# An FFT filter with a top-128 feed-forward: x kept by halves of the channels, VectorE without folds and weight splits, a new order

## The chip, the cores and the metric

The kernel runs on one core of a Trainium2 chip. The metric is the device time in microseconds (us) of one execution.

## The reference

`x` is [8, 3136, 256] in f32: 8 batches, 3136 tokens, 256 channels. All in f32:

```
X = rfft(x, axis=1);  Y = X * (filt_r + 1j*filt_i);  y = irfft(Y)
scores = y @ w_gate                             # one per token
for each batch: idx = the 128 tokens of the highest score
  xe = y[idx]; ye = relu(xe @ w1) @ w2          # 256 -> 1024 -> 256
  y[idx] = xe + sigmoid(scores[idx]) * ye
```

## The kernel before, in words

**The transform.** 3136 = 98 * 32, and the FFT is done as two small DFTs by matmul. The tile `X` holds one batch, 98 rows (on 113 partitions: two groups of 49, at partitions 0 and 64) by 32 by 256 channels. It is the only such tile: it takes the loaded `x`, and later the result `y` of the batch before, in halves of 128 channels. The work is staged thus, with the names of the code:

- `load` (SP, lines 591 to 598): one half of `x` from DRAM, in two DMAs, of 112 partitions (L595) and of the one that is left (L596).
- the fold (L435): the symmetry of the DFT is used by forming sum and difference of two halves of a row, for one chunk of 32 channels at a time, 8 chunks a batch. The string `FOLD` has for each batch and chunk two letters, for the sum and for the difference: `p` on GpSimd (POOL), `d` on VectorE (DVE), `x` no fold: TensorE (PE) adds both operands in PSUM, with two more matmuls.
- `amm` (PE, L461): DFT over the 98. `tout` (DVE, L465): a 32x32 transpose out of PSUM into the tile `UU`.
- `inner`, for 13 pairs of rows: `zmm` (PE, L364) DFT over the 32; `zout` (ScalarE, ACT, L382) and `pmul` (DVE, L386), `qmul` (POOL, L389): product with the filter tables `fa_sb` and `fb_sb`; `vmm` (PE, L373): the inverse with `ti_sb`; `vout` (ACT, L398) back into `UU`; `gate` (DVE, L404): the scores.
- `tin` (DVE, L426) transposes back, `ymm` (PE, L567) is the last inverse DFT, `yout` (ACT, L570) writes into `X`, `store` (SP, L584, L587, L589) writes a half to DRAM.

`inner` of batch t runs beside the way out of batch t-1 and the way in of batch t+1. So a half of `X` is written by `yout`, stored, loaded anew and folded, in a ring.

**The selection** (`select`) finds the 128 tokens of a batch by 8 rounds of counting: ACT counts (L675), PE adds up (L684), and `over` works out the next bound, on ACT (L698, L699) or, where `SELM` of the batch is 1, on DVE (L692, L694).

**The feed-forward** (`ffn`) gathers the tokens, in four groups of batches; three of the groups multiply with weights in two f32r parts. The parts are made in 8 pieces, the upper by ACT (L872), the lower by a subtraction (L875) on POOL for the pieces in `WPOOL`, else on DVE. At the end indirect DMAs on POOL write the rows back (L987).

**Start.** The filter tables arrive in four parts (`PARTS`, L1040) and are copied to a second set of partitions by `spread` (L1047) on the engines in `SPR`; `turn_ti` (L1074, L1076) makes the second half of `ti_sb`. `warmup` (L1068) issues 2 * 34 matmuls on zeros (`WARM=34`).

**What sets the order.** Every step is appended to `prog` by `op(when, engine, cost, fn, reads, writes)`, but only the list `ORDER` counts: the steps are issued in its order (L1147), and each engine and SP's queue run theirs in that order, waiting on semaphores where a step needs data. `when`, `cost` and `lat` are a planner's figures (us); the kernel itself doesn't use them.

Of the kernel before, what the change touches and what calls it, by code (L numbers as in the profile page):

```python
# [9 lines left out]
F32 = mybir.dt.float32  # L10
# [7 lines left out]
B, S, D, FF = 8, 3136, 256, 1024  # L18
# [26 lines left out]
def _tables(C):  # L45
# [45 lines left out]
    for r in range(8):  # L91
# [10 lines left out]
    ti = ti.transpose(4, 1, 2, 3, 0, 5).reshape(128, NPR * 128)  # L102
# [20 lines left out]
    ],  # L123
    BACK=["ffffffff", "ffffffff", "ffffffff", "ffffffff", "ffffffff", "ffffffff", "peqeqqhq", "ppppffff"],
    BRING=["yyzzzzza", "yyzyzyza", "yyzzzzya", "aazzavza", "yyzzyvza", "aazzyyzy", "aaaaaaaa", "azvazava"],
    YRING=[
        "yymyyymyyyyyyyyy",
        "yyyyyyyyyyyyyyyy",
        "yyyyyyyyyyyyyyyy",
        "yyyyyyyyyyyyyyyy",  # L130
        "yyyyyyyyyyyyyyyy",
        "yyyyymyyyyyyyymy",
        "myymyymyyymymmym",
        "mmmymymyyyyyyymy",
# [3 lines left out]
        ["act", "pool", "act", "dve"],  # L138
        ["pool", "pool", "dve", "dve"],
        ["pool", "act", "dve", "dve"],  # L140
    ],
    SELM=[0, 0, 0, 0, 0, 1, 1, 1],
    WPOOL=[3, 6, 1, 4, 2],
# [105 lines left out]
]  # L249


# [928 lines left out]
```

## Time and profile before

| | us |
|---|---|
| median of 3 runs | 499.3 (492.7 to 499.85) |
| the profiled execution | 495.63 |
| its span, first to last instruction | 493.8 |

The rows below come from the profiled execution. Busy time is what the profiler records for each engine; matmul ends are modelled. A line number is that of the kernel before. In the span's first 60 us the first batches and the tables come in, to about 372 us the batches follow each other in a period of about 45 us, and the rest is the last way out, the last selections and the feed-forward.

### The profile page before, as it was taken

To read this page: it belongs to the slowest core of one execution; us is meant where nothing else is said; L and a number is where in the kernel's file an instruction comes from. 1 tells how busy PE (TensorE), PEld (TensorE's weight loads), DVE (VectorE), ACT (ScalarE), POOL (GpSimd) and SP (SyncE) were. 2 spreads that over 40 slices of the span, in tenths; PEclk is the share of its full clock that TensorE was granted. 3 is DMA by queue.
4 is the path that set the end of the run, shared out by engine and by line. 5 is a ranking of instruction groups with operands and counts; after the bars stand their busy time and mean duration, and the time that the engine had idled before them with its cause. 6 is when DMAs were issued, how large, how long until landed. Compare 5 with 4: busy or idle time off the path is not lost.

```text
span 493.8 us, 10471 instructions
## 1 busy us (share of the span) xinstructions
PE 439.3 (89%) x3876; PEld 223.3 (45%) x3876; DVE 404.7 (82%) x1062; ACT 276.9 (56%) x665; POOL 303.0 (61%) x257
## 2 busy tenths in 40 slices
PE   4847788999799999999999899989997979699996
PEld 4214342543244434343443244424433545368995
DVE  0699987999598989898999888989998997857642
ACT  1243423678356677457766675757666558466320
POOL 0678888663667459656966677657864654652023
PEclk9698998999899999999999999999999999899999
DMA  9999386117682828474758384758222465416411
GB/s 193 255 294 218 75 177 145 42 49 192 173 182 78 201 70 203 98 204 102 180 138 205 91 195 105 195 141 210 75 72 69 128 152 170 127 34 143 140 44 44
DMA packets 116856, 69.22 MB, mean 140 GB/s; under 512 B 3782, under 2 KB 115142, under 8 KB 116550
## 3 DMA queue, kind: packets, MB, share of 16 engines
q1 hardware_dynamic: 116038, 66.46, 55.9%
q0 software_dynamic: 768, 2.10, 1.3%
q8 instruction: 31, 0.51, 0.4%
q14 instruction: 19, 0.16, 0.1%
HBM read 41.61 MB, written 26.94 MB: 139 GB/s over the span
## 4 chain that ended last, share of the span: by engine, by line
PE 44%; DVE 18%; DMA 13%; issue 7%; POOL 7%; ACT 3%; SPq 0%; POOLq 0%; DVEq 0%; ACTq 0%
PE pv L373 12%; PE py L567 11%; DMA X<-in_x_dram 11%; PE pa L461 6%; PE pz L364 6%; DVE rj L404 5%; DVE y L386 3%; DVE t L426 2%; POOL q L389 2%; DMA out_dram<-X 2%; DVE UU L465 2%; POOL s L435 2%; POOL X L435 2%; ACT UU L398 1%; POOL out_dram L987 1%
## 5 line engine op out<-in xcount | busy, mean ns | idle before, releaser
L389 POOL TENSOR_TENSOR q<-q,fb_sb 128x512 f32<-128x512 f32 (+1 forms) x104 | 135.2, 1317 | 54.5 <-ACT q L382 51.2
L567 PE MATMUL py<-t,c_sb 128*98 128x512 f32 x198 | 109.0, 633 | 3.2 <-ACT X L570 2.9
L435 POOL TENSOR_TENSOR s<-X 113x512 f32<-113x512 f32 x48 | 63.2, 1325 | 70.3 <-DMA X<-in_x_dram 60.6
L404 DVE SCALAR_TENSOR_TENSOR rj<-pv,wg_sb 128x256 bf16<-128x256 f32 x200 | 83.8, 419 | 12.4 <-ACT UU L398 4.4
L461 PE MATMUL pa<-X,c_sb 49*64 49x512 f32 x320 | 77.6, 647 | 10.9 <-DMA c_sb<-in_cst_dram 5.6
L398 ACT COPY UU<-pv 128x512 f32<-128x512 f32 x96 | 51.7, 589 | 57.9 <-PE pv L373 57.4
L426 DVE STREAM_TRANSPOSE t<-UU 128x1024 f32<-128x1024 f32 x64 | 78.7, 1231 | 4.0 <-PE pm L684 3.4
L465 DVE STREAM_TRANSPOSE UU<-pa 128x1024 f32<-128x1024 f32 x59 | 73.2, 1240 | 6.9 <-PE pa L461 6.7
L570 ACT COPY X<-py 98x512 f32<-98x512 f32 x99 | 57.6, 582 | 36.7 <-PE py L567 15.8
L373 PE MATMUL pv<-y,ti_sb 64*64 64x256 f32 x800 | 68.2, 389 | 9.6 <-DVE rj L404 8.2
L382 ACT COPY q<-pz 128x512 f32<-128x512 f32 (+1 forms) x104 | 56.7, 585 | 30.2 <-PE pz L364 28.8
L364 PE MATMUL pz<-UU,tf_sb 64*64 64x256 f32 x800 | 61.8, 406 | 11.5 <-DVE y L386 8.3
L386 DVE TENSOR_TENSOR y<-pz,fa_sb 128x512 f32<-128x512 f32 (+1 forms) x104 | 67.5, 673 | 3.3 <-ACT q L382 3.2
L373 PE MATMUL pv<-q,ti_sb 64*64 64x256 f32 x800 | 66.1, 378 | 0.0
L435 POOL TENSOR_TENSOR X<-X 113x512 f32<-113x512 f32 x46 | 59.1, 1288 | 6.8 <-DVE s L435 5.5
L461 PE MATMUL pa<-s,c_sb 49*64 49x512 f32 x216 | 58.9, 618 | 4.0 <-POOL s L435 2.2
L364 PEld LDWEIGHTS pz<-UU,tf_sb 64*64 64x64 f32 x800 | 28.5, 134 | 51.1 <-issue 20.6
L373 PEld LDWEIGHTS pv<-y,ti_sb 64*64 64x64 f32 x800 | 29.5, 134 | 47.3 <-issue 15.9
L567 PEld LDWEIGHTS py<-t,c_sb 128*98 128x98 f32 x198 | 25.4, 166 | 42.4 <-ACT X L570 12.6
L373 PEld LDWEIGHTS pv<-q,ti_sb 64*64 64x64 f32 x800 | 34.6, 134 | 11.4 <-issue 0.2
L675 ACT ACTIVATE junk<-R,nb 128x392 bf16<-128x392 f32 x48 | 29.8, 622 | 12.7 <-DVE nb L694 12.2
L461 PEld LDWEIGHTS pa<-X,c_sb 49*64 49x64 f32 x320 | 18.5, 139 | 27.2 <-POOL X L435 7.3
(202 smaller groups left out, 590.0 us busy)
## 6 DMA issues: line engine op xcount, KB each, us to landing
X<-in_x_dram SPq DMA_DIRECT2D x16, 1792.0 KB
out_dram<-X SPq DMA_DIRECT2D x13, 1568.0 KB
out_dram<-X SPq DMA_DIRECT2D x12, 384.0 KB
R<-scr SPq DMA_DIRECT2D x16, 196.0 KB
fb_sb<-in_moe_w_dram SPq DMA_DIRECT2D x2, 1024.0 KB
ti_sb<-in_ti_dram SPq DMA_DIRECT2D x1, 832.0 KB
tf_sb<-in_tf_dram SPq DMA_DIRECT2D x1, 800.0 KB
fa_sb<-in_fri_dram SPq DMA_DIRECT2D x2, 320.0 KB
```

Source lines behind the costliest of these rows:

```text
L364: nc.tensor.matmul(half(z, k)[o, hi], lhsT=tf_sb[p, l], rhs=urow(b, l, 0, D)[p], start=True, stop=True)
L373: nc.tensor.matmul(half(v, k)[o, j], lhsT=ti_at[p, t, i, hi], rhs=y[p, hi], start=t == 0, stop=t == 1)
L382: nc.scalar.copy(out=q[:np_], in_=half(h["z"], k)[:np_])
L386: nc.vector.tensor_tensor(out=y[:np_], in0=half(h["z"], k)[:np_], in1=fa_sb[:np_, i], op=ALU.mult)
L389: nc.gpsimd.tensor_tensor(out=h["q", k][:np_], in0=h["q", k][:np_], in1=fb_sb[:np_, i], op=ALU.mult)
L404: nc.vector.scalar_tensor_tensor(out=rj, in0=half(h["v"], k)[:, j], scalar=1.0, in1=wg_sb, op0=ALU.mult, op1=ALU.mult, accum_out=urow(b, l ...
L426: nc.vector.transpose(out=h["t"].rearrange("p d (l j) -> p d l j", j=2), in_=uchan(b_out, c))
L435: (nc.gpsimd if fold[k] == "p" else nc.vector).tensor_tensor(out=out, in0=two[0], in1=two[1], op=(ALU.add, ALU.subtract)[k])
L461: nc.tensor.matmul(a[o, w].rearrange("p (n d) -> p n d", d=CW), lhsT=lhs[p], rhs=rhs[p], start=n == 0, stop=n == len(terms) - 1)
L465: nc.vector.transpose(out=uchan(b_in, c), in_=h["a"].rearrange("p w (n d) -> p d n w", d=CW))
L567: nc.tensor.matmul(yp[:N1], lhsT=cc["wi"][:, :N1], rhs=h["t"][:, n * CY:(n + 1) * CY].rearrange("p a b -> p (a b)"), start=True, stop=True)
L570: nc.scalar.copy(out=X[:N1, :, at], in_=e["y"][:N1])
```

## The change

- In DRAM and in `X` the channels are split in two halves as an outer axis, [.., 2, 32, 128] in place of [.., 32, 256], so a half that is loaded is one run of 16 KB on each partition, on both sides, where it was 32 runs of 512 B. The output in DRAM keeps its layout: a store still writes runs of 512 B.
- `FOLD` has no `d` any more: 18 `d` become 9 more `p` (103 in place of 94) and 9 more `x` (25 in place of 16). `WPOOL` has all 8 pieces: DVE's three go to POOL. One chunk of batch 6 goes out by `p` in place of `h` (one step less on DVE, one more on ACT and on POOL).
- Batches 2 and 4 have `SELM` 1. Two of the table copies go from POOL to ACT. The PSUM banks of some steps change.
- The planner's figures change: a load costs 5.8 in place of 6.8, copies on DVE more; a step `boot` issues nothing. The host makes `ti` in two halves, of which the first is loaded, as before; that a DMA could bring table copies or the second half of `ti_sb` is provided for, but no entry of `SPR` or `TIM` asks for it.
- `ORDER` is new as a whole. The number of warming matmuls, `WARM=34`, stands in both kernels.

```diff
@@ -99,7 +99,8 @@
     tf = np.stack([tf[h, :, :, :, :, h] for h in range(2)]).reshape(128, L, 64)
     ti = np.stack([ti[:, h, :, :, h] for h in range(2)])
     ti = np.concatenate([ti, ti[:, :, :, -1:]], 3).reshape(2, 2, K2, NPR, 2, 64)
-    ti = ti.transpose(4, 1, 2, 3, 0, 5).reshape(128, NPR * 128)
+    ti = ti.transpose(4, 1, 2, 3, 0, 5).reshape(2, 2, 32, NPR * 128)
+    ti = np.stack([ti, np.stack([-ti[:, 1], ti[:, 0]], 1)], 3).reshape(128, 2, NPR * 128)
...
@@ -112,35 +113,36 @@
     AO6=0, AO7=0, SD=0, WARM=34, FR=0.2, F0=41.542, G7=0, KEEP=6.362,
 
     FOLD=[
-        "xp pp dp dx pp dd xx pd",
-        "pp xx xx xx xp dp dp pp",
-        "pp pp pp pp pd xx pp dp",
-        "pp dp pp xp pp pd xp xp",
-        "pp pd pp pp pp pp pd pp",
-        "pp pp dp pp pp pp dp pp",
-        "pd dp pp pp pp pp pp pp",
-        "pp pp pp dp pp pp pp pp",
+        "xx pp pp px px pp xp pp",
+        "pp xx xp pp xp xx pp px",
+        "xx pp xp pp pp xx pp pp",
+        "pp pp pp xp pp pp xp xp",
+        "pp px pp pp pp pp pp pp",
+        "pp pp pp pp xx pp pp pp",
+        "pp pp pp pp pp pp xp pp",
+        "pp pp pp pp pp px pp pp",
     ],
-    BACK=["ffffffff", "ffffffff", "ffffffff", "ffffffff", "ffffffff", "ffffffff", "peqeqqhq", "ppppffff"],
-    BRING=["yyzzzzza", "yyzyzyza", "yyzzzzya", "aazzavza", "yyzzyvza", "aazzyyzy", "aaaaaaaa", "azvazava"],
+    BACK=["ffffffff", "ffffffff", "ffffffff", "ffffffff", "ffffffff", "ffffffff", "peqeqqpq", "ppppffff"],
+    BRING=["yyazzzya", "yyzzzzya", "yazayvza", "ayzzzzva", "yazayvza", "yyazzzya", "aaaaaaaa", "azvazava"],
     YRING=[
-        "yymyyymyyyyyyyyy",
+        "yymyyymyyyyymyyy",
+        "yyyyyyyyyymyyyyy",
         "yyyyyyyyyyyyyyyy",
-        "yyyyyyyyyyyyyyyy",
-        "yyyyyyyyyyyyyyyy",
+        "yyyyyyyyyyymyyyy",
         "yyyyyyyyyyyyyyyy",
         "yyyyymyyyyyyyymy",
-        "myymyymyyymymmym",
-        "mmmymymyyyyyyymy",
+        "mymyyyyyymmmmyym",
+        "ymyyyymyyyyyyymy",
     ],
     SPR=[
         ["pool", "act", "dve", "dve"],
-        ["act", "pool", "act", "dve"],
-        ["pool", "pool", "dve", "dve"],
+        ["act", "act", "act", "dve"],
+        ["pool", "act", "dve", "dve"],
         ["pool", "act", "dve", "dve"],
     ],
-    SELM=[0, 0, 0, 0, 0, 1, 1, 1],
-    WPOOL=[3, 6, 1, 4, 2],
+    TIM=["dve", "act", "dve", "act"],
+    SELM=[0, 0, 1, 0, 1, 1, 1, 1],
+    WPOOL=[0, 1, 2, 3, 4, 5, 6, 7],
     PARTS=[(0, 2), (2, 4), (4, 8), (8, 13)],
     ALONE=[["a", "z", "v"], ["a"]],
...
 ORDER = [
-    1, 4, 2, 3, 49, 57, 53, 50, 59, 54, 60, 55, 51, 52, 15, 58, 61, 56, 62, 20, 35, 38, 36, 39, 18, 46, 16, 40, 37, 5,
...
+    2, 0, 5, 3, 4, 56, 52, 57, 49, 58, 53, 21, 50, 59, 54, 51, 36, 60, 55, 38, 16, 61, 39, 46, 62, 6, 37, 24, 42, 40,
...
@@ -289,8 +290,8 @@
     late = {}
     fb_sb = const.tile([128, NPR, 2, D], F32, name="fb_sb")
     fb_rows = fb_sb.rearrange("p i h d -> p (i h) d")
-    X = const.tile([128, N2, D], F32, name="X")
-    Xh = X.rearrange("p (h n) d -> p h n d", h=2)
+    X = const.tile([128, 2, N2, D // 2], F32, name="X")
+    Xh = X.rearrange("p t (h n) d -> p t h n d", h=2)
...
@@ -427,8 +428,8 @@
 
             fold = FOLD[b_in].split()[c] if b_in < B else "--"
 
-            at = slice(c * CW, c * CW + CW)
-            two = Xh[:RW2, 0, :, at], Xh[:RW2, 1, :, at]
+            at = slice(o, o + CW)
+            two = Xh[:RW2, hx, 0, :, at], Xh[:RW2, hx, 1, :, at]
             apart = "x" in fold
...
                 h["a"] = a = psum[pa].tile([128, 2, 512], F32, name="p" + pa)
                 for k in range(2):
                     if fold[k] == "x":
-                        terms = [(cc["wa"][:, 64 * k:64 * k + 64], Xh[:, 0, :, at]),
-                                 (cc["wn"] if k else cc["wa"][:, :64], Xh[:, 1, :, at])]
+                        terms = [(cc["wa"][:, 64 * k:64 * k + 64], Xh[:, hx, 0, :, at]),
+                                 (cc["wn"] if k else cc["wa"][:, :64], Xh[:, hx, 1, :, at])]
                     else:
-                        terms = [(cc["wa"][:, 64 * k:64 * k + 64], h["s"] if apart or k == 0 else Xh[:, 1, :, at])]
+                        terms = [(cc["wa"][:, 64 * k:64 * k + 64], h["s"] if apart or k == 0 else Xh[:, hx, 1, :, at])]
...
 
-                def yout(e=e, at=slice(g * CY, g * CY + CY)):
-                    nc.scalar.copy(out=X[:N1, :, at], in_=e["y"][:N1])
+                def yout(e=e, hx=hx, at=slice(o + n * CY, o + (n + 1) * CY)):
+                    nc.scalar.copy(out=X[:N1, hx, :, at], in_=e["y"][:N1])
...
@@ -581,21 +582,20 @@
             at = slice(h * HD, h * HD + HD)
             for w in range(2):
                 for k in range(2):
-                    nc.sync.dma_start(out=ow[b, w, k, :48, :, at], in_=Xh[64 * w:64 * w + 48, k, :, at])
+                    nc.sync.dma_start(out=ow[b, w, k, :48, :, at], in_=Xh[64 * w:64 * w + 48, h, k])
             for w in range(2):
                 for k in range(2):
-                    nc.sync.dma_start(out=ow[b, w, k, 48:49, :, at], in_=Xh[64 * w + 48:64 * w + 49, k, :, at])
+                    nc.sync.dma_start(out=ow[b, w, k, 48:49, :, at], in_=Xh[64 * w + 48:64 * w + 49, h, k])
             return
-        nc.sync.dma_start(out=ov[b, :, :, h * HD:(h + 1) * HD], in_=X[:N1, :, h * HD:(h + 1) * HD])
+        nc.sync.dma_start(out=ov[b, :, :, h * HD:(h + 1) * HD], in_=X[:N1, h])
 
     def load(when, b, h, bias=0.0):
         def f():
             if b < B:
-                at = slice(h * HD, h * HD + HD)
-                nc.sync.dma_start(out=X[:112, :, at], in_=x[b, :112, :, at])
-                nc.sync.dma_start(out=X[112:RW2, :, at], in_=x[b, 112:, :, at])
+                nc.sync.dma_start(out=X[:112, h], in_=x[b, :112, h])
+                nc.sync.dma_start(out=X[112:RW2, h], in_=x[b, 112:, h])
         n = HD // CW
-        op(when, "sp", 6.8 if b < B else .01, f, (), [("x", h, c) for c in range(h * n, h * n + n)], lat=2, bias=bias)
+        op(when, "sp", 5.8 if b < B else .01, f, ["boot"], [("x", h, c) for c in range(h * n, h * n + n)], lat=2, bias=bias)
...
@@ -1043,6 +1043,9 @@
 
         a, b = PARTS[i]
         t = (fa_sb, fb_sb)[k]
+        if eng == "sp":
+            nc.sync.dma_start(out=t[64 * w + 32:64 * w + 64, a:b], in_=fri[k, 32 * w:32 * w + 32, a:b])
+            return
         copy = dict(dve=nc.vector.tensor_copy, pool=nc.gpsimd.tensor_copy, act=nc.scalar.copy)[eng]
         copy(out=t[64 * w + 32:64 * w + 64, a:b], in_=t[64 * w:64 * w + 32, a:b])
...
     def turn_ti(w, k):
 
         re, im = slice(64 * w, 64 * w + 32), slice(64 * w + 32, 64 * w + 64)
-        if k == 0:
+        to = (im, re)[k]
+        if TIM[2 * w + k] == "sp":
+            nc.sync.dma_start(out=ti_sb[to, 1], in_=ti[to, 1])
+        elif k == 0:
             nc.vector.tensor_copy(out=ti_sb[im, 1], in_=ti_sb[re, 0])
         else:
             nc.scalar.activation(out=ti_sb[re, 1], in_=ti_sb[im, 0], func=AF.Copy, scale=-1.0)
...
+    op(-120, "sp", 1.7, lambda: None, (), ["boot"])
...
     op(-87.9, "sp", .5, lambda: raw_in(128, 0, NCUT), (), [*held, "raw1"], lat=2)
-    op(-87.8, "dve", .2, lambda: raw_out(128, 0, NCUT), [*held, "raw1"], ["c"])
...
             for w in range(2):
                 eng = SPR[i][2 * k + w]
-                op(when, eng, dict(dve=.06 + .27 * n, act=.2 + .43 * n, pool=.3 + .43 * n)[eng], lambda i=i, k=k, w=w, eng=eng: spread(i, k, w, eng),
-                   [("fa" "fb"[2 * k:2 * k + 2] + "r", i)], [("fa" "fb"[2 * k:2 * k + 2], i)])
-    op(TIO, "sp", 3.4, lambda: nc.sync.dma_start(out=ti_sb[:, 0], in_=ti), (), ["ti0"], lat=2)
+                op(when, eng, dict(dve=.2 + .4 * n, act=.2 + .43 * n, pool=.3 + .43 * n, sp=.24 * n)[eng], lambda i=i, k=k, w=w, eng=eng: spread(i, k, w, eng),
+                   ["boot"] if eng == "sp" else [("fa" "fb"[2 * k:2 * k + 2] + "r", i)], [("fa" "fb"[2 * k:2 * k + 2], i)], lat=2 * (eng == "sp"))
+    op(TIO, "sp", 3.4, lambda: nc.sync.dma_start(out=ti_sb[:, 0], in_=ti[:, 0]), ["boot"], ["ti0"], lat=2)
     for w in range(2):
-        op(TIO + .1, "dve", .95, lambda w=w: turn_ti(w, 0), ["ti0"], ["ti"])
-        op(TIO + .1, "act", 1.5, lambda w=w: turn_ti(w, 1), ["ti0"], ["ti"])
+        for k in range(2):
+            eng = "sp" if TIM[2 * w + k] == "sp" else ("dve", "act")[k]
+            op(TIO + .1, eng, dict(dve=1.35, act=1.5, sp=.85)[eng], lambda w=w, k=k: turn_ti(w, k), ["boot"] if eng == "sp" else ["ti0"], ["ti"],
+               lat=2 * (eng == "sp"))
...
@@ -1166,7 +1175,7 @@
     tokens = data["x"].reshape(B, 2, NH, N2 // 2, 2, D)
     for w in range(2):
         xs[:, 64 * w:64 * w + NH] = tokens[:, :, :, :, w].transpose(0, 2, 1, 3, 4)
-    data["x"] = xs.reshape(B, RW2, N2, D)
+    data["x"] = np.ascontiguousarray(xs.reshape(B, RW2, N2, 2, D // 2).transpose(0, 1, 3, 2, 4))
```

## Rows read from the trace of the kernel before

**Rows 1.** The page, parts 1 and 5: busy us of each engine; a group, its mean ns

```profile
PE 439.3 (89%) x3876; PEld 223.3 (45%) x3876; DVE 404.7 (82%) x1062; ACT 276.9 (56%) x665; POOL 303.0 (61%) x257
...
L435 POOL TENSOR_TENSOR s<-X 113x512 f32<-113x512 f32 x48 | 63.2, 1325 | 70.3 <-DMA X<-in_x_dram 60.6
```

**Rows 2.** Stretches: length, busy us of PE, PEld, DVE, ACT, POOL; clock, DMA share, GB/s

```profile
60.00:372.00 312.00, 295.40 (x2667) 127.33 (x2667) 278.69 (x737) 195.96 (x498) 214.20 (x171) 0.99 0.57 139
...
428.00:467.00 39.00, 38.56 (x219) 30.20 (x220) 25.52 (x108) 21.07 (x51) 9.66 (x11) 0.92 0.42 105
```

**Rows 3.** The chain that ended last, in order of time: start us, us, what

```profile
117.27 9.74 DMA X<-in_x_dram
...
241.27 10.78 DMA X<-in_x_dram
...
314.77 11.10 DMA X<-in_x_dram
```

**Rows 4.** Who waited for whom: us in total, times, longest us

```profile
POOL s L435 <- DMA X<-in_x_dram: 60.6, 11, 11.0
```

**Rows 5.** By stretch: one load of x; then the loads of moe weights

```profile
118.00:126.00 8.00, 7.28 (x36) 2.18 (x34) 7.48 (x19) 5.98 (x19) 1.26 (x1) 1.00 1.05 231
...
406.00:408.00 2.00, 1.74 (x32) 1.46 (x32) 2.00 (x6) 1.91 (x5) 1.27 (x1) 1.00 1.01 397
408.00:410.00 2.00, 2.00 (x14) 0.67 (x9) 1.84 (x7) 1.55 (x3) 0.00 (x0) 1.00 1.03 373
```

**Rows 6.** In order of time, the queue on SP: start us, us, instruction

```profile
1.58 5.15 SPq L596 DMA_DIRECT2D X<-in_x_dram  x1
...
8.03 6.76 SPq L596 DMA_DIRECT2D X<-in_x_dram  x1
```

**Rows 7.** In order of time, the first 36 us: VectorE and GpSimd

```profile
11.92 1.77 POOL L435 TENSOR_TENSOR s<-X 113x512 f32<-113x512 f32 x1 [10.99 <-DMA X<-in_x_dram]
...
18.76 1.25 DVE L465 STREAM_TRANSPOSE UU<-pz 128x1024 f32<-128x1024 f32 x1 [1.47 <-PE pz L461]
...
20.82 2.48 POOL L435 TENSOR_TENSOR s<-X 113x512 f32<-113x512 f32 x2 [4.25 <-DMA X<-in_x_dram]
...
29.39 1.21 DVE L465 STREAM_TRANSPOSE UU<-pv 128x1024 f32<-128x1024 f32 x1
30.62 4.41 DVE L1047 COPY fb_sb<-fb_sb 32x2048 f32<-32x2048 f32 x2
...
35.07 0.69 DVE L386 TENSOR_TENSOR y<-pz,fa_sb 128x512 f32<-128x512 f32 x1
```

**Rows 8.** Groups of instructions by line and shape, VectorE: busy us, mean ns of one

```profile
L435 DVE TENSOR_TENSOR s<-X 113x512 f32<-113x512 f32 x11 | 9.4, 858 | 13.4 <-DMA X<-in_x_dram 13.4
L435 DVE TENSOR_TENSOR X<-X 113x512 f32<-113x512 f32 x7 | 9.4, 1343 | 3.2 <-POOL s L435 3.2
...
L694 DVE TENSOR_SCALAR nb<-J,nd 128x1 f32<-128x1 f32 x24 | 5.1, 214 | 0.9
...
L692 DVE TENSOR_SCALAR_CACHE_REDUCE ok<-pm 128x15 f32<-128x15 f32 x16 | 2.4, 150 | 3.9 <-PE pm L684 3.9
```

**Rows 9.** The chain again: matmul groups of the first DFT of x

```profile
138.46 1.02 PE pa L461 x8
...
149.41 1.70 PE pa L461 x12
```

**Rows 10.** Groups by line and shape, ScalarE: a strided write, a contiguous one

```profile
L570 ACT COPY X<-py 98x512 f32<-98x512 f32 x99 | 57.6, 582 | 36.7 <-PE py L567 15.8 <-POOL q L389 6.4 <-PE pm L684 3.9
L382 ACT COPY q<-pz 128x512 f32<-128x512 f32 x96 | 52.1, 586 | 28.3 <-PE pz L364 27.3 <-POOL q L389 0.7
```

**Rows 11.** In order of time, 418 to 432 us: VectorE, then ScalarE, then TensorE

```profile
421.79 5.20 DVE L875 TENSOR_TENSOR fa_sb<-fb_sb,fa_sb 128x512 fp32r<-128x512 f32 x1
...
428.68 0.62 ACT L675 ACTIVATE junk<-R,nb 128x392 bf16<-128x392 f32 x1 [4.59 <-DVE nb L694]
...
428.41 1.98 PE L495 MATMUL pv<-t,c_sb 64*64 64x512 f32 x8 [4.50 <-DVE ok L692]
```

More of the change, by code (lines that the diff above doesn't have):

```diff
@@ L258 @@
         PLAN[k] for k in ("P CO SO RT ST P7 TC7 C7 C8 S7 FL FG FC FI FD F7 TS TC0 X0 XA RW TIO FH LAT I0 LG LS SW SW7 BS7 AI7 AO6 AO7 SD WARM FR F0 G7 KEEP").split())
-    (FOLD, BACK, BRING, YRING, SPR, SELM, WPOOL, PARTS, ALONE, TRING, URING, DRING, FGRP, BUFS) = (
-        PLAN[k] for k in "FOLD BACK BRING YRING SPR SELM WPOOL PARTS ALONE TRING URING DRING FGRP BUFS".split())
+    (FOLD, BACK, BRING, YRING, SPR, SELM, WPOOL, PARTS, ALONE, TRING, URING, DRING, TIM, FGRP, BUFS) = (
+        PLAN[k] for k in "FOLD BACK BRING YRING SPR SELM WPOOL PARTS ALONE TRING URING DRING TIM FGRP BUFS".split())
     nc = tc.nc
@@ L447, in outer, with amm @@
             pa = "a" if b_out >= 0 else ALONE[b_in][c % len(ALONE[b_in])]
-            def amm(h=h, pa=pa, at=at, fold=fold, apart=apart):
+            def amm(h=h, pa=pa, at=at, hx=hx, fold=fold, apart=apart):
                 h["a"] = a = psum[pa].tile([128, 2, 512], F32, name="p" + pa)
@@ L539, in outer @@
                 pb = BRING[b_out][c]
-                ats = [slice((2 * c + n) * CY, (2 * c + n + 1) * CY) for n in range(2)]
+                ats = [slice(o + n * CY, o + (n + 1) * CY) for n in range(2)]
                 def ymm2(h=h, pb=pb):
@@ L549, in ymm2, with yout2 @@
                         nc.tensor.matmul(h["e"][n][:N1], lhsT=cc["wi"][:, :N1], rhs=h["t"][:, n * CY:(n + 1) * CY].rearrange("p a b -> p (a b)"), start=True, stop=True)
-                def yout2(n, h=h, ats=ats):
-                    nc.scalar.copy(out=X[:N1, :, ats[n]], in_=h["e"][n][:N1].rearrange("p (d n) -> p n d", n=N2))
+                def yout2(n, h=h, ats=ats, hx=hx):
+                    nc.scalar.copy(out=X[:N1, hx, :, ats[n]], in_=h["e"][n][:N1].rearrange("p (d n) -> p n d", n=N2))
                 E_ = [("y", "E", b_out, c), ("m", "E", b_out, c)] if pb == "y" else [(pb, "E", b_out, c)]
@@ L1084 @@
         op(-99.5, "pe", .2 * WARM, warmup, (), (), new=("m", "warm"))
-    op(-99, "sp", .3, lambda: nc.sync.dma_start(out=c_sb[:, :192], in_=cst[:, NCUT:NCUT + 192]), (), ["wa"], lat=2)
+    op(-99, "sp", .3, lambda: nc.sync.dma_start(out=c_sb[:, :192], in_=cst[:, NCUT:NCUT + 192]), ["boot"], ["wa"], lat=2)
     for h in range(2):
@@ L1091 @@
     op(-87.9, "sp", .5, lambda: raw_in(128, 0, NCUT), (), [*held, "raw1"], lat=2)
-    op(-87.8, "dve", .2, lambda: raw_out(128, 0, NCUT), [*held, "raw1"], ["c"])
+    op(-87.8, "dve", .6, lambda: raw_out(128, 0, NCUT), [*held, "raw1"], ["c"])
     CO, C7, SO = (max(v, 7.2 - P / NPR) for v in (CO, C7, SO))
```

185 rows, old and new, of the table ORDER are left out of this document.

## The prediction

> **What bounds the kernel now.** I read the page's sums first: TensorE (PE) is busy for 89% of the span and VectorE (DVE) for 82%, GpSimd (POOL) for 61% [rows 1]. Averages hide the stages, so next the table by stretches. From 60 to 372 us PE is busy for 295.4 of 312 us and DVE for 278.7: by the records PE stands idle for 16.6 us there, DVE for 33.3, and in the tail from 428 to 467 us PE lacks 0.4 us [rows 2]. The reader is to see that no saving in the middle can exceed PE's idle time, and that what is won ahead of 428 us passes through a full PE to the end. Then the chain of waits: from 107 to 326 us it runs five times through a load of x, each 10 to 11 us long (the first of them, one between and the last stand in the group) [rows 3], so the ring of store, load and fold sets part of the pace. The waits agree from POOL's side: its folds stood 60.6 us for x, 11 times [rows 4], and as POOL takes its queue in order, the products with the filter behind a fold stand as well. Last the order of time at the two ends. The start is a chain of transfers: SP needs 5.15 and 6.76 us to issue the single-partition piece of a load, as it is held behind the large piece [rows 6], and the folds begin at 11.92 us, those of the other half at 20.82 us [rows 7]. In the tail there is one VectorE instruction of 5.20 us, after which both ScalarE (ACT) and PE had been waiting for 4.5 us [rows 11].
>
> **The load.** A half is 1,792 KB, or 1.835 MB. While one load ran alone, in runs of 512 B, 231 GB/s were moved with the DMA engines always busy; the feed-forward weights, in runs of 1 and 4 KB, came at 397 and 373 GB/s, with the engines as busy [rows 5]. So 1.835 MB take 7.9 us now, and 4.8 us at 385 GB/s: 3.2 us less a load. The trace has no run of 16 KB; the bounds are nothing (as now) and 1.835 MB at 397, 3.3 us. I take 3.2, as the weight loads are the nearest rows in kind, long runs from DRAM. Stores keep runs of 512 B in DRAM: no term.
>
> [...]
>
> **The start.** x's first half lands 3.2 us earlier and the second 6.4: folds can begin at 8.7 and 14.4 us. All folds of batch 0 but five are now POOL's: 11 by 1.33 us [rows 1] are 14.6 us in a row, to 23.3 us, and some 2 us more, as POOL's fold took 1.77 us beside a fold on DVE [rows 7] and DVE's table copies will run beside it. After the last fold come its matmuls and two transposes: the last transpose ends near 27 us, where it ended at 30.6. DVE, which had the five `d` folds and then 4.41 us of copies ahead of its first filter product at 35.07 us [rows 7], is now free between the transposes and does those copies there; the product can start near 28. Between 3.5 us (the last transpose) and 9 us (6.4 of transfers, and 2.6 for half of DVE's five folds, each 1.04 us, as 18 took 18.8 [rows 8]) I take **-7**: the product is what PE waited for. On SP, the tables keep their place behind x, with parts 1 and 2 exchanged and the constants (308 KB, 0.8 us) now ahead of batch 1's second half; the loads there are each 3.2 us shorter.
>
> **The middle.** DVE loses 13 `d` folds of 1.04 us, 13.5 us, and gets the rounds of batches 2 and 4: 16 by 0.15 + 0.21 us, 5.8 [rows 8]; net -7.7, over some 330 us. PE gets eight `x` (the ninth is in the start): two more matmuls each are half of 1.70 - 1.02, 0.34 us [rows 9], in all 2.7 us. POOL gets five folds in batches 1 to 7, 6.6 us; it is busy for 214 of 312 us [rows 2], so this is hidden, as long as the fold isn't the last thing that PE waits for. A load that is 3.2 us shorter takes that much from waits of 5.5 us on average [rows 4]: 0.58 of 16.6 us, 9.6, if all PE's idle time were x's. Bounds: +2.7 (only the matmuls are felt) and -13.9 (all idle time goes). I take **-4.5**: 9.6 - 2.7 is 6.9, of which about two thirds, since PE's idle time has other causes too. When the load is in time, the next to be late are DVE's transposes. On SP the scores of batch 5 are now written ahead of a store, as those of 3 and 4 were before, so a late selection holds that store.
>
> **The tail.** The 5.20 us are a subtraction of two SBUF operands. It goes to POOL with two others, 3 by about 1.3 us, and POOL is busy there for 9.7 of 39 us [rows 2]. PE's wait of 4.50 us [rows 11] goes; behind it PE is full, so all of it counts. Bounds 0 (POOL late with a weight piece) and -4.5: I take **-4**.
>
> **No term.** ACT's copies into `X` with a step between elements take 582 ns, and contiguous ones 586 [rows 10], so a smaller step in `X` costs nothing. Two table copies go from POOL to ACT, which idles in the start; the PSUM banks and the chunk of batch 6 move single steps of 0.6 to 1.3 us between engines with room. `boot` issues nothing, the second half of `ti` isn't loaded, and the warming matmuls are as many as before: of that part of the change nothing is in the code.
>
> **The sum.** -7 - 4.5 - 4 = -15.5 against the profiled execution's 495.63 us, of which 493.8 are span: 480.1, so **480 us**. That execution lies 0.7% under the median of 499.3, inside the runs shown. A measurement of this kernel can tell about 2%, 10 us, from no change.
>
> **The rivals.** *The load is no faster.* Runs of 512 B remain if the DMA is cut as before, or DRAM sets the rate. Then the start keeps only half of DVE's five folds, -2.6, the middle nothing, the tail -4: 489. Against it are the weight loads at 385 GB/s. Chance 0.18. *The ring sets the pace everywhere.* Five loads on the chain by 3.2 are 16 us, and the middle gives 12 of its 13.9: 495.6 - 7 - 12 - 4 = 472.6, some 473. For it speaks the chain; against it that PE is busy for 95% of the middle. Chance 0.15. *Slower: an order for loads that come too late.* The planner counts 5.8 us and 2 of latency for a load, where it counted 6.8, so the new order puts folds and matmuls 1 us closer behind each load. In queues that run in order that is a wait for PE at each of 14 loads if they still take 9.7 to 11 us [rows 3]: 495.6 + 14 - 4 = 505.6. It decides from the point where issue to landing exceeds 7.8 us; by the load's term it is near 6.8. Chance 0.12.
>
> **How the numbers follow.** The forecast has 0.55, with its own range 473 to 487 (the bounds of the start and half of those of the middle). The range 470 to 491 takes in the first two rivals and leaves out the third and some edge. Faster by over 2%: 0.53 of the forecast, 0.15, and a third of the first rival (0.05), 0.73; slower by over 2%: most of the third, 0.10; within 2% the rest, 0.17.
>
> **What would show it.** Right: a load is landed some 7 us after its issue and moves over 350 GB/s; SP issues the single-partition piece in under 1 us; POOL's first folds stand near 8.7 and 14.4 us and DVE's first filter product near 28; no VectorE instruction of 5 us near 410, and PE without the wait of 4.5 us behind it; PE's idle time in the middle nearer 10 than 16.6 us. Wrong: loads still at 230 GB/s; POOL's folds, now nearly alone in their work, as what PE waits for in the middle; or the 7 us of the start gone by 110 us, because DVE was the slower there.

## The result, and the profile after

The kernel after takes 480.02 us (median of 4 runs, 475.69 to 482.31), the kernel before in the same runs 496.56: a ratio of 0.966, 95% interval 0.955 to 0.977. The profiled execution took 480.46 us, with a span of 478.7. Ratios, and the medians of the table below, leave out the executions of a slower state, in which a kernel takes over 1.5% longer than its fastest execution; the profiled one of before was marked so, but its 495.63 us and its granted clock of 0.967 lie among the fast ones that came later (490.8 to 498.8 us, 0.957 to 0.974). The time came out as forecast; the way to it did not. The page's sums, against [rows 1]: DVE has lost 19.5 us and POOL gained 6, PE's busy time is as it was.

```profile
PE 438.4 (92%) x3912; PEld 224.7 (47%) x3912; DVE 385.2 (80%) x1088; ACT 271.8 (57%) x620; POOL 309.0 (65%) x268
```

**Where the time went.** I cut both spans at two stores that both kernels issue: the first half of batch 0 and the first half of batch 5. First, of before: the length of the stretch, busy us of PE, PEld, DVE, ACT, POOL, then clock, DMA share and GB/s.

```profile
107.11:353.55 246.44, 235.61 (x2063) 99.55 (x2059) 219.18 (x578) 161.39 (x419) 165.66 (x133) 0.99 0.62 151
353.55:493.80 140.25, 122.93 (x1004) 83.45 (x996) 101.88 (x334) 72.67 (x168) 63.67 (x67) 0.97 0.39 104
0.00:107.11 107.11, 80.75 (x821) 40.31 (x825) 83.63 (x152) 42.84 (x79) 73.69 (x58) 0.90 0.72 162
```

The same three stretches of the kernel after:

```profile
106.72:344.30 237.58, 229.52 (x2051) 98.07 (x2047) 212.34 (x607) 151.51 (x369) 167.63 (x137) 1.00 0.58 157
344.30:478.70 134.40, 122.00 (x1032) 82.84 (x1024) 97.54 (x337) 74.28 (x171) 67.70 (x71) 0.99 0.41 109
0.00:106.72 106.72, 86.88 (x837) 43.80 (x841) 75.35 (x146) 46.01 (x81) 73.72 (x61) 0.89 0.62 162
```

The start gave 0.4 us, the middle 8.9, the tail 5.85: together 15.1. The terms had been 7, 4.5 and 4. So all three were wrong in size, and that they made up for each other was luck.

**The load.** The chain of waits of after, in order of time (start us, us, what), against the 10 to 11 us of [rows 3]:

```profile
116.24 8.86 DMA X<-in_x_dram
258.94 8.97 DMA X<-in_x_dram
307.08 9.49 DMA X<-in_x_dram
```

Two stretches of after in which one load runs alone, against 231 GB/s in [rows 5]:

```profile
118.00:124.00 6.00, 6.00 (x32) 1.78 (x24) 5.45 (x13) 4.36 (x14) 0.00 (x0) 1.00 0.92 259
260.00:266.00 6.00, 5.87 (x33) 1.90 (x31) 5.76 (x17) 4.74 (x15) 0.95 (x1) 1.00 0.96 262
```

A load is some 1.4 us shorter (mean of three, 10.5 to 9.1), not 3.2, and the last column stands at 260, not at 385. What came out as forecast is SP's queue at the start of after: the single-partition piece of L596 is issued in 0.3 us, where [rows 6] had 5.15 and 6.76.

```profile
0.75 0.40 SPq L595 DMA_DIRECT2D X<-in_x_dram  x1
1.21 0.31 SPq L596 DMA_DIRECT2D X<-in_x_dram  x1
1.97 0.48 SPq L595 DMA_DIRECT2D X<-in_x_dram  x1
2.49 0.33 SPq L596 DMA_DIRECT2D X<-in_x_dram  x1
```

**The start.** In order of time, POOL and DVE of after, beside [rows 7]:

```profile
10.58 3.69 POOL L436 TENSOR_TENSOR s<-X 113x512 f32<-113x512 f32 x3 [9.65 <-DMA X<-in_x_dram]
...
19.57 1.26 POOL L436 TENSOR_TENSOR s<-X 113x512 f32<-113x512 f32 x1 [1.54 <-DMA X<-in_x_dram]
...
29.38 1.21 DVE L466 STREAM_TRANSPOSE UU<-pv 128x1024 f32<-128x1024 f32 x1
...
33.86 1.29 DVE L387 TENSOR_TENSOR y<-pz,fa_sb 128x512 f32<-128x512 f32 x2 [0.97 <-DMA fa_sb<-in_fri_dram]
```

The halves stand ready at 10.58 and 19.57 us (forecast 8.7 and 14.4), so the last transpose is where it was, and the product starts at 33.86, not near 28; it waited 0.97 us for the DMA of a table, and the DMA share is 1.02 from 20 to 32 us. POOL's wait for x only fell from 60.6 [rows 4] to 56.2 us:

```profile
POOL s L436 <- DMA X<-in_x_dram: 56.2, 10, 9.9
```

**The tail.** DVE has no instruction of 5 us any more, and PE issues the matmul that had waited 4.50 us [rows 11] without a wait. In order of time:

```profile
414.14 2.54 POOL L875 TENSOR_TENSOR fa_sb<-fb_sb,fa_sb 128x512 fp32r<-128x512 f32 x2
...
416.62 1.13 PE L496 MATMUL pv<-t,c_sb 64*64 64x512 f32 x8
416.62 1.31 POOL L875 TENSOR_TENSOR ti_sb<-fb_sb,ti_sb 128x512 fp32r<-128x512 f32 x1
```

### The profile page after: what moved, and what is told of

The parts are those of the page before. It is cut to its first block, busy times and chain, and to the rows that moved or that the text cites. A ratio compares the mean times of both kernels' runs of the same rounds, so it can differ in the third digit from the quotient of the medians.

```text
span 478.7 us, 10501 instructions
## 1 busy us (share of the span) xinstructions
PE 438.4 (92%) x3912; PEld 224.7 (47%) x3912; DVE 385.2 (80%) x1088; ACT 271.8 (57%) x620; POOL 309.0 (65%) x268
## 4 chain that ended last, share of the span: by engine, by line
PE 46%; DMA 25%; DVE 10%; POOL 8%; issue 7%; ACT 3%; SPq 0%; POOLq 0%; ACTq 0%; DVEq 0%
PE pv L374 12%; DMA X<-in_x_dram 11%; PE py L568 11%; PE pa L462 8%; DMA out_dram<-X 7%; PE pz L365 5%; DVE rj L405 4%; DMA fb_sb<-in_fri_dram 3%; POOL s L436 2%; DMA R<-scr 2%; POOL q L390 2%; POOL X L436 2%; DMA fa_sb<-in_fri_dram 2%; DVE y L387 1%; ACT UU L399 1%
## 5 line engine op out<-in xcount | busy, mean ns | idle before, releaser
L390 POOL TENSOR_TENSOR q<-q,fb_sb 128x512 f32<-128x512 f32 (+1 forms) x104 | 132.4, 1289 | 70.0 <-ACT q L383 63.1
L436 POOL TENSOR_TENSOR s<-X 113x512 f32<-113x512 f32 x58 | 73.4, 1273 | 56.3 <-DMA X<-in_x_dram 56.2
L568 PE MATMUL py<-t,c_sb 128*98 128x512 f32 x192 | 104.2, 625 | 3.9 <-ACT X L571 3.7
L462 PE MATMUL pa<-X,c_sb 49*64 49x512 f32 x356 | 81.5, 611 | 6.8 <-DMA c_sb<-in_cst_dram 3.8
L571 ACT COPY X<-py 98x512 f32<-98x512 f32 x96 | 56.0, 583 | 38.8 <-PE py L568 17.2
L374 PE MATMUL pv<-y,ti_sb 64*64 64x256 f32 x800 | 69.9, 392 | 7.2 <-DVE rj L405 6.0
L374 PE MATMUL pv<-q,ti_sb 64*64 64x256 f32 x800 | 69.0, 382 | 0.6 <-DVE fb_sb L1050 0.6
L462 PE MATMUL pa<-s,c_sb 49*64 49x512 f32 x212 | 56.7, 605 | 2.6 <-DVE UU L466 2.2
L436 POOL TENSOR_TENSOR X<-X 113x512 f32<-113x512 f32 x45 | 57.3, 1275 | 1.6
L462 PEld LDWEIGHTS pa<-X,c_sb 49*64 49x64 f32 x356 | 20.7, 135 | 24.4 <-issue 9.6
```

The costliest lines, as they stand in the source:

```text
L374: nc.tensor.matmul(half(v, k)[o, j], lhsT=ti_at[p, t, i, hi], rhs=y[p, hi], start=t == 0, stop=t == 1)
L390: nc.gpsimd.tensor_tensor(out=h["q", k][:np_], in0=h["q", k][:np_], in1=fb_sb[:np_, i], op=ALU.mult)
L436: (nc.gpsimd if fold[k] == "p" else nc.vector).tensor_tensor(out=out, in0=two[0], in1=two[1], op=(ALU.add, ALU.subtract)[k])
L462: nc.tensor.matmul(a[o, w].rearrange("p (n d) -> p n d", d=CW), lhsT=lhs[p], rhs=rhs[p], start=n == 0, stop=n == len(terms) - 1)
L568: nc.tensor.matmul(yp[:N1], lhsT=cc["wi"][:, :N1], rhs=h["t"][:, n * CY:(n + 1) * CY].rearrange("p a b -> p (a b)"), start=True, stop=True)
```

## The experiments

My theory at this point: the halves gave the middle, the split gave the tail, and a load has a limit other than the length of its runs. Rivals: the new order, or DVE's freed time, gave the middle; packets of 16 KB are themselves slow; x's place in DRAM is. The ratio is to the kernel before in the same set of runs; start, middle and tail are the three stretches above, each read from the one profiled execution of its run, so their sum can lie some 3 us off the median.

| run | median us | ratio (95%) | start | middle | tail |
|---|---|---|---|---|---|
| before | 493.5 to 496.6 | 1 | 107.1 | 246.4 | 140.2 |
| after | 480.0 | 0.966 (0.955 to 0.977) | 106.7 | 237.6 | 134.4 |
| after, old layout of x | 487.7 | 0.983 (0.978 to 0.989) | 106.7 | 246.9 | 134.4 |
| before, halves only | 484.3 | 0.978 (0.973 to 0.982) | 106.0 | 237.4 | 139.3 |
| after, load in 4-KB runs | 478.3 | 0.969 (0.963 to 0.974) | 103.9 | 237.6 | 134.6 |
| after, three splits on DVE | 481.4 | 0.973 (0.966 to 0.979) | 106.2 | 237.7 | 135.4 |
| after, load of 128 partitions | 470.4 | 0.953 (0.947 to 0.959) | 99.3 | 231.1 | 138.6 |
| before, halves, no split | 478.3 | 0.968 (0.963 to 0.974) | 108.6 | 238.3 | 132.9 |
| the same, no fold on DVE | 481.9 | 0.975 (0.970 to 0.981) | 111.7 | 238.2 | 132.9 |
| after, 80 warming matmuls | 483.0 | 0.977 (0.973 to 0.982) | 109.0 | 238.1 | 137.0 |
| before, halves, no split, 128 partitions | 470.9 | 0.953 (0.947 to 0.958) | 104.4 | 234.5 | 132.8 |
| after, 128 rows in DRAM, load of 112 | 479.5 | 0.967 (0.962 to 0.972) | 106.2 | 237.5 | 134.4 |
| after, old layout, load of 128 | 486.5 | 0.982 (0.976 to 0.987) | 104.0 | 244.2 | 136.0 |
| after, load in 2 x 64 partitions | 506.6 | 1.020 (1.012 to 1.028) | 112.5 | 257.9 | 134.4 |

How far equal code differs from one profiled execution to the next: the starts of runs 2 and 6 (106.0 and 108.6) and the tails of after and run 8 (134.4 and 137.0) have the same steps in the same order and differ by 2.6 us. The middle is steadier: the eight kernels with halves and loads of 112 partitions lie between 237.4 and 238.3. So a difference under 3 us in a start or a tail is not told apart from chance.

**1. The halves taken back.** The kernel after, with the layout of before and all the rest changed:

```diff
-    X = const.tile([128, 2, N2, D // 2], F32, name="X")
+    X = const.tile([128, N2, D], F32, name="X")
...
-                nc.sync.dma_start(out=X[:112, h], in_=x[b, :112, h])
+                nc.sync.dma_start(out=X[:112, :, at], in_=x[b, :112, :, at])
```

> The changed kernel with x back in runs of 512 B, in DRAM and in the tile; order, folds and weight splits stay those of the change. Theory L (the halves made the middle faster: each load 1.2 us shorter, and SP free 5 us earlier): the 9 us won between 80 and 344 us are mostly lost, 487 to 490 us. Theory O (the order and the relief of VectorE made the middle faster): 481 to 483 us, although every load takes 10 us again.

487.7 us: theory L. The middle is that of before again, 246.9, the tail that of after. With loads this long, DVE's 7.7 us and the new order together gave nothing in the middle.

**2. The halves alone**, the same edit the other way round in the kernel before.

> The kernel before with nothing but the halves: x in runs of 16 KB, old order, old folds, old splits. Theory L: 486 to 490 us. Theory O: the old order can't use loads that are 1.2 us shorter, 494 to 497 us. Both: SP's issue of the single-partition piece falls from 5.4 us to 0.3, and a load lands about 8.9 us after its issue.

484.3 us, beyond what theory L gave: the middle is 237.4, all of what the full change won there, in the old order and with DVE's 18 folds. What is missing is the tail. Its rows, in order of time:

```profile
410.42 1.28 POOL L874 TENSOR_TENSOR ti_sb<-fb_sb,ti_sb 128x512 fp32r<-128x512 f32 x1
411.13 6.00 DVE L874 TENSOR_TENSOR fa_sb<-fb_sb,fa_sb 128x512 fp32r<-128x512 f32 x1
411.67 1.26 POOL L874 TENSOR_TENSOR tf_sb<-fb_sb,ti_sb 128x512 fp32r<-128x512 f32 x1
412.90 2.46 POOL L526 TENSOR_TENSOR X<-X,s 113x512 f32<-113x512 f32 x2
415.33 1.25 POOL L874 TENSOR_TENSOR fa_sb<-fb_sb,fa_sb 128x512 fp32r<-128x512 f32 x1
...
418.55 1.99 PE L495 MATMUL pv<-t,c_sb 64*64 64x512 f32 x8 [4.79 <-DVE ok L691]
```

DVE's split starts while POOL is in a row of two-operand instructions, and ends at 417.13, 0.55 us after the last of them (415.33 + 1.25).

**3. Is it the size of a run?** The load of after in four DMAs of 4 KB a partition:

```diff
-                nc.sync.dma_start(out=X[:112, h], in_=x[b, :112, h])
+                for q in range(4):
+                    s = slice(q * N2 // 4, (q + 1) * N2 // 4)
+                    nc.sync.dma_start(out=X[:112, h, s], in_=x[b, :112, h, s])
```

> The changed kernel with each load cut in four DMAs of 4 KB a partition, same bytes, same layout. Theory P (the size of the runs sets the rate: 16 KB packets took 972 ns each, 16.9 GB/s an engine, packets of 4 KB 172 ns, 23.8 GB/s): a load moves at 370 GB/s or more, lands some 7 us after issue, x's second half is there at 15 to 16 us in place of 19.6, and the kernel takes 474 to 478 us. Theory M (something else holds the rate, the 112 partitions over the 16 DMA engines or DRAM): 260 GB/s and 8.9 us as before, and 480 us.

Theory M by the rate; the time, 478.3 us, is not told apart from after. The two loads below move at 280 GB/s, and from the first issue (112.51) to the landing (114.32 + 7.40 on the chain) it is 9.2 us.

```profile
114.00:120.00 6.00, 6.00 (x30) 1.96 (x30) 4.79 (x12) 4.83 (x15) 0.00 (x0) 1.00 1.02 280
257.00:263.00 6.00, 5.87 (x33) 1.90 (x31) 5.72 (x17) 4.70 (x14) 0.90 (x1) 1.00 1.02 281
```

**4. Splits on DVE in the new order.** `WPOOL=[3, 6, 1, 4, 2]` in the kernel after.

> The changed kernel with the weight pieces 0, 5 and 7 split on VectorE again, as before the change; the order stays new. Theory S (VectorE waits while GpSimd runs): one or two VectorE subtractions of 2 to 5 us between 405 and 420 us, the last selection later by about as much, 483 to 486 us. Rival: in the new order they fall where GpSimd is idle, 0.7 us each, and the time stays at 480 us; then the 7.5 us won in the last selection are the order's.

The rival: 481.4 us, not told apart from after. The same instruction takes 0.69 us, as POOL isn't in such work when it starts:

```profile
412.38 0.69 DVE L875 TENSOR_TENSOR tf_sb<-fb_sb,ti_sb 128x512 fp32r<-128x512 f32 x1
414.39 0.69 DVE L875 TENSOR_TENSOR fa_sb<-fb_sb,fa_sb 128x512 fp32r<-128x512 f32 x1
414.96 1.28 POOL L875 TENSOR_TENSOR fa_sb<-fb_sb,fa_sb 128x512 fp32r<-128x512 f32 x1 [2.89 <-ACT fa_sb L872]
```

So what the tail had paid for was where the split met POOL, not that it was on DVE.

**5. A load of 128 partitions.** The weight loads that my rate came from have 128 partitions, the load of x has 112 and one apart. In the kernel after, with x padded to 128 rows:

```diff
-                nc.sync.dma_start(out=X[:112, h], in_=x[b, :112, h])
-                nc.sync.dma_start(out=X[112:RW2, h], in_=x[b, 112:, h])
+                nc.sync.dma_start(out=X[:, h], in_=x[b, :, h])
...
-    xs = np.zeros((B, RW2, 2, N2 // 2, D), np.float32)
+    xs = np.zeros((B, 128, 2, N2 // 2, D), np.float32)
```

> The changed kernel, with x padded in DRAM from 113 to 128 rows per batch, so that a half is one DMA of 128 partitions by 16 KB (2.10 MB, 14% more bytes than the piece of 112 partitions), and no single-partition piece. All the rest as changed. Theory Q (how the partitions fall on the 16 DMA engines holds the rate: with 112 partitions the 16-KB packets went at 16.9 GB/s an engine, with 128 partitions the forward tables went at 25): a load moves near 385 GB/s and is landed some 7.4 us after its issue instead of 9; the second half of the first x is there near 16 us instead of 19.6; the store milestones run ahead of the changed kernel's from batch 0 on; 470 to 476 us. Theory R (it is x's place in DRAM or its own pattern of reads, not the number of partitions): still 17 GB/s an engine, 260 to 275 GB/s, 9.5 to 10.5 us from issue to landing, and as there are 14% more bytes the time is 479 to 484 us.

Theory Q: 470.4 us, with run 9 the best of all. The stretches of two loads:

```profile
110.50:116.00 5.50, 5.50 (x31) 1.65 (x27) 5.34 (x13) 4.33 (x14) 0.00 (x0) 1.00 0.96 372
153.50:159.00 5.50, 5.50 (x56) 2.83 (x52) 5.06 (x13) 3.33 (x10) 2.00 (x2) 1.00 1.00 380
```

With 14% more bytes a load is landed 7.4 us after its issue (SP at 109.46, POOL's fold below at 116.83). The start, POOL and DVE in order of time, is now what the prediction had worked out:

```profile
8.24 3.70 POOL L436 TENSOR_TENSOR s<-X 113x512 f32<-113x512 f32 x3 [7.31 <-DMA X<-in_x_dram]
...
28.59 1.29 DVE L387 TENSOR_TENSOR y<-pz,fa_sb 128x512 f32<-128x512 f32 x2 [0.90 <-ACT q L383]
...
116.83 1.27 POOL L436 TENSOR_TENSOR s<-X 113x512 f32<-113x512 f32 x1 [8.93 <-DMA X<-in_x_dram]
```

**6. Halves and no split, in the old order:** the halves in the kernel before, and `WPOOL=[0, 1, 2, 3, 4, 5, 6, 7]`.

> The kernel before, in its old order and with its old folds, with two parts of the change: x by halves in DRAM and in the tile, and all weight splits of the feed-forward stage on GpSimd. Theory S (the 4.5-us stall of PE behind VectorE's split was worth its length, and the halves gave the rest): the VectorE instruction of 5 to 6 us near 411 is gone, PE has no wait of over 1 us there, and the time is that of the halves alone, 484.3, less 4 to 6: 478 to 480 us, no slower than the full change. Theory O (the new order is what wins in the tail: in the old one GpSimd brings the last weight pieces late and PE waits for those): 482 to 485 us.

Theory S: 478.3 us, no slower than the full change. Against run 2 the tail is 6.4 us shorter, and nothing but the three splits was moved. The two tails, run 2 and run 6; then the clock behind PE's wait in run 2:

```profile
343.43:482.70 139.27, 122.24 (x1004) 83.49 (x996) 102.82 (x334) 72.75 (x168) 64.51 (x68) 0.97 0.39 105
346.98:479.90 132.92, 119.92 (x1004) 81.98 (x996) 95.64 (x331) 72.65 (x168) 67.22 (x70) 1.00 0.41 110
...
418.00:424.00 6.00, 5.45 (x20) 3.11 (x20) 4.06 (x12) 2.49 (x6) 0.98 (x1) 0.59 0.11 29
```

**7. The same without folds on DVE:** each `d` of `FOLD` made `p`.

> The kernel before, in its old order, with all three parts of the change that touch an engine's work: halves, no fold on VectorE (each d of the fold table made p), all weight splits on GpSimd. Not taken over: the new order, the new choice of x folds, the selections of batches 2 and 4, the tables. Against the run with VectorE's folds left in, it tells what those 18 folds are worth. Theory S (VectorE isn't what PE waits for in the middle): 477 to 481 us, within 2 us of the kernel that keeps them. Theory V (VectorE's work in the middle is what paces, as my forecast took for part of its 4.5 us): 4 to 8 us faster than with the folds kept. Third: GpSimd, which now makes all folds in an order that was written for both, is late for PE: 483 to 488 us.

481.9 us, between what theory S and the third gave it. Beside run 6 the middle is the same (238.2 and 238.3), so DVE's folds cost the middle nothing. The start is 3.1 us longer, little more than the 2.6 us between equal starts, and the intervals overlap: that POOL's making all folds costs the start anything is not shown.

**8. More warming matmuls,** which the change names and its code lacks: `WARM=80` in the kernel after.

> The changed kernel with 80 warming matmuls instead of 34: the part 'more warming matmuls' that its words name and its code doesn't have. If the clock at the first transposes and filter products matters (the granted clock is 0.5 to 0.6 between 12 and 20 us), 1 to 2 us less: 478 to 479. If not, as PE waits for transfers there: 480, no difference that can be measured, and the stores of batch 0 at the same time as before within 1 us.

483.0 us: no gain; the intervals of the two kernels overlap, so a loss is not shown either. The clock is the column before the last two. Of this run, then of the kernel after:

```profile
8.00:20.00 12.00, 9.40 (x104) 5.45 (x106) 3.63 (x3) 0.00 (x0) 7.68 (x7) 1.00 0.98 249
20.00:32.00 12.00, 10.39 (x51) 2.83 (x43) 6.26 (x6) 5.37 (x5) 8.75 (x6) 0.57 1.03 292
```

```profile
8.00:20.00 12.00, 8.02 (x41) 2.61 (x45) 2.87 (x3) 0.00 (x0) 7.80 (x7) 0.72 1.00 255
20.00:32.00 12.00, 7.52 (x65) 2.77 (x58) 10.42 (x9) 5.37 (x5) 8.57 (x6) 0.90 1.02 284
```

The slow clock isn't avoided: it comes later, when PE has idled 2.16 us for the second half of x, and lies on the transposes' matmuls of that half; the last transpose starts at 31.87 instead of 29.38 us.

**9. The version that the runs pointed to:** run 6 with the load of run 5.

> The version that the runs so far point to: the kernel before in its old order and with its old folds, with the halves, all weight splits on GpSimd, and a load of a half as one DMA of 128 partitions (x padded to 128 rows a batch in DRAM). Theory N (the new order is worth nothing, as the old order with halves and no split came to 0.968 of the time before and the full change to 0.966): the 128-partition load gives the old order as much as it gave the new one, some 10 us: 467 to 471 us. Theory W (the new order, planned for a load of 5.8 us, is worth something once loads are that fast): 473 to 477 us.

Theory N: 470.9 us, the same as run 5. The new order isn't needed for it. The two differ by stretch, however: run 5 is ahead by 5 us in the start and by 3 in the middle, and loses 6 in the tail. Of these 6, 1.5 stand between after and run 6 as well (134.4 and 132.9). In its trace run 5 has a granted clock of 0.57 from 380 to 384 us and a wait of PE of 1.49 us near 449 us (L948, for `y` of L962), neither of which after has; why they come is open. The start of the one with the tail of the other was not run.

**10. Rows of DRAM or partitions?** Run 5 had changed both. Here x is padded as in run 5 and loaded as in the change (112 partitions and one).

> The changed kernel with x padded to 128 rows a batch in DRAM, but each half loaded as the change does, 112 partitions and one apart. It separates the two things that the run of one DMA of 128 partitions changed at once. Theory P (the number of partitions in the DMA sets the rate): 255 to 265 GB/s with the engines busy, about 9 us from issue to landing, 478 to 482 us, as the changed kernel. Theory D (where the rows lie in DRAM sets it): 370 GB/s or more, landed some 7 us after the issue, 470 to 474 us.

Theory P: as the kernel after, in time and in rate:

```profile
117.00:123.00 6.00, 6.00 (x33) 1.83 (x31) 5.40 (x13) 4.84 (x15) 0.00 (x0) 1.00 0.93 270
259.50:265.50 6.00, 5.87 (x33) 1.90 (x31) 5.71 (x17) 4.70 (x14) 0.90 (x1) 1.00 0.89 262
```

One thing is not separated: wherever 112 partitions were loaded, the single-partition piece went along, and 112 without it were not run.

**11. Runs of 512 B with 128 partitions:** run 1's layout, one DMA `out=X[:, :, at], in_=x[b, :, :, at]`.

> The changed kernel with x in the old layout (rows of both halves, runs of 512 B) but loaded as one DMA of 128 partitions from a padded x. The halves alone were worth 7.4 us with 112 partitions. Theory A (both limits exist: long runs and 128 partitions are needed): loads at 250 to 320 GB/s, 8 us or more from issue to landing, 474 to 483 us. Theory B (the partitions are the whole of it, and the halves were a detour): 370 GB/s or more, 470 to 473 us, as with halves and 128 partitions.

Theory A, and slower than I gave it: 486.5 us, no better than run 1. Four loads ran at 254 to 282 GB/s, one of which is below; neither long runs alone (259 to 270 with 112 partitions) nor 128 partitions alone reach the 370 to 380 of both (run 5).

```profile
232.00:240.00 8.00, 8.00 (x71) 3.51 (x67) 7.33 (x25) 4.58 (x10) 7.64 (x7) 1.00 0.99 254
```

**12. Two DMAs of 64 partitions** in place of run 5's one.

> The changed kernel with x padded to 128 rows in DRAM and each half loaded in two DMAs of 64 partitions. Theory M (an engine is slow when its share of the partitions is 7 and not a power of two, so 4 each are as good as 8): the two together at 370 GB/s or more, landed some 7.5 to 8 us after the first issue, 470 to 473 us. Theory F (the full 128 partitions at once are needed): 180 to 300 GB/s, 9 us or more, 478 to 484 us.

Theory F by its rate, though the time is far above what I gave it: 506.6 us, 1.2 to 2.8% slower than the kernel before. Two loads, and how long such a load stands on the chain:

```profile
123.50:132.50 9.00, 8.45 (x52) 2.77 (x50) 8.01 (x20) 6.57 (x21) 0.00 (x0) 1.00 0.99 213
227.00:236.00 9.00, 7.73 (x67) 3.17 (x66) 8.39 (x26) 4.42 (x9) 0.00 (x0) 1.00 0.99 216
```

```profile
122.05 11.97 DMA X<-in_x_dram
225.64 11.95 DMA X<-in_x_dram
```

## Why the prediction was right, and where it was not

**The load (-3.2 a load) failed, and with it the start.** The step took 385 GB/s from the weight loads as "the nearest rows in kind, long runs from DRAM". They were near in one respect only. Runs 3, 5, 10 and 12 show the other: with long runs, 64 partitions in a DMA gave 208 to 216 GB/s, 112 gave 256 to 281, 128 gave 370 to 380 (360 to 395 in run 9). In place of -3.2 us a load lost 1.4.

Run 12's two DMAs of 64 partitions stood 11.97 and 11.95 us on the chain, where the 112 and one of the kernel after stood 8.86 to 9.49. Why 112 come slower than 128, and 64 slower still, stays open. The length of the runs told as well, both at 128 partitions: 254 to 282 GB/s with 512 B (run 11), 370 to 380 with 16 KB (run 5).

**The start (-7): measured -0.4.** Its working was right on a wrong input. With the rate that it assumed (run 5) folds begin at 8.24, the product at 28.59, and the stretch is 7.4 us shorter than in the kernel after. The old order, in which DVE keeps its folds, has 104.4 us with such loads (run 9), where run 5 has 99.3.

**The middle (-4.5): measured -8.9,** all of it from the halves (run 2: -9.0; run 1, without them: +0.4), none from DVE, as runs 1 and 7 show. The step that failed is the first reading: "no saving in the middle can exceed PE's idle time", after which the term was made as a share of that time. As a bound it held (8.9 of the 10.8 us that PE is idle between the two stores), but most of the saving was not idle time. That fell only to 8.1 us, and from 60 to 372 us from 16.6 to 14.1, not to the 10 that the prediction named. The step also took a load's 3.2 us: with the 1.4 us that a load lost, its working gives 1.4/5.5 of 16.6, less 2.7, and two thirds of that, 1.0 us. So the 4.5 came as near as it did by luck. What fell as well is PE's busy time: run 2, with the same 2063 matmuls as before, is busy for 229.28 us there, before for 235.61.

```profile
106.01:343.43 237.42, 229.28 (x2063) 98.11 (x2059) 221.19 (x578) 161.53 (x419) 164.14 (x132) 1.00 0.58 157
```

Part of this is the clock: in before, PE stands still for lack of folds near 130 us (waits of 1.55 and 0.27 us for POOL's two folds), and then works at a granted clock of 0.81 and 0.76. In order, of before:

```profile
128.00:132.00 4.00, 2.76 (x8) 0.39 (x8) 2.80 (x9) 0.56 (x2) 3.92 (x4) 0.81 0.78 215
132.00:136.00 4.00, 3.40 (x12) 1.30 (x14) 1.03 (x5) 0.83 (x4) 4.00 (x4) 0.76 0.65 190
```

That is 1.7 us of full speed (0.19 and 0.24 of 4 us); in run 2 and in the kernel after, no such stretch of 4 us is below 0.99 in the middle. Where the other 4.6 us were is open; the busy times of run 2 and run 7, whose 2063 matmuls take middles of 237.4 and 238.2 us, differ by 3.3 us (229.28 and 232.57). So PE's waits near 130 us cost more in before than their idle time shows, by the clock behind them at least, and the busy share understated what the ring was worth: with ten loads in the middle, 0.9 us came out per load of the 1.4 saved.

**The tail (-4): measured -5.85.** The mechanism was right, the size too small: run 2 against run 6 gives 6.4 for the three splits alone. Of these, 4.0 are PE's idle time (17.0 to 13.0), as forecast. The other 2.3 are its busy time, with the same 1004 matmuls (122.24 to 119.92): behind the wait PE worked at a granted clock of 0.59 from 418 to 424 us, and in run 6 the granted clock is 1.00 from 410 to 450 us. The wait was counted, the slow clock behind it was not, though [rows 2] have a clock of 0.92 over the 39 us behind the wait in before.

**SP's queue, the strides, the other moves** (no term) came out as said: ACT's copy into `X` takes 583 ns after, and runs 1 and 2 leave nothing in the middle for the new order, the tables or the selections.

**The rivals.** "The load is no faster" was nearer on the rate, but its price (nothing in the middle) was not: 1.4 us a load sufficed. "The ring sets the pace" described the middle (-8.9 of its -12). "An order for loads that come too late" fell: run 1 has the new order with loads of 9.6 to 10.7 us on the chain and takes 487.7 us, not 505.6. Whether it would hold for longer loads is not shown: run 12 has 12 us in the new order only.

So 480 was right by luck, by a sum of three wrong sizes: 6.6 us too much in the start, 4.4 too little in the middle, 1.9 too little in the tail.

## What to carry to other kernels

Take a transfer's rate from a row with the same number of partitions and the same length of run: here it needed both 128 partitions and long runs (370 to 380 GB/s in run 5; with one of the two 254 to 282), and padding 113 rows to 128 made the time 1.4 to 1.6% shorter by the ratios (runs 5 and 9 beside after and run 6) at 14% more bytes. Cut the span at the same events in both kernels before explaining a time that came out as forecast: a right sum says little of its terms. Read the clock beside the busy share: PE was full in the tail, at 0.92. And before moving an instruction of 5 us to another engine, ask what it takes where nothing holds it: 0.69 us here.

## What the hardware showed that I had not expected

- With a DMA share of 0.89 to 1.0, 16-KB runs came at 208 to 216 GB/s (64 partitions, run 12), 259 to 270 (112, after and run 10) and 370 to 380 (128, run 5). So the share says nothing about the rate here.
- A VectorE instruction of two SBUF operands, 0.65 to 0.69 us by itself, took 5.20 us in before and 6.00 in run 2: it ended 0.56 and 0.55 us after the last of a row of two-operand GpSimd instructions, and didn't get in between two of them. The wait lasted over four of GpSimd's instructions in before and five in run 2; what held it is not shown.
- 92 more warming matmuls (run 8) moved the first stretch at a low clock (granted 0.56 and 0.59 from 12 to 20 us in the kernel after) to 20 to 32 us (0.57), and did not remove it.
